# Attention followed by two MLPs: the first weight's conversion is spread differently, and one small addition changes engine

## The chip, the cores and the metric

The kernel runs on one core of a Trainium2 chip. The metric is the device time of one execution in microseconds (us). The kernel before took 933.87 us (median of three runs, 932.76 to 934.47). The profile shown here belongs to one execution that took 932.79 us.

The core has four compute engines with a queue of instructions each, and each works through its own queue in order: TensorE (PE; its weight loads are listed as PEld), VectorE (DVE), ScalarE (ACT) and GpSimd (POOL). SyncE (SP) only issues transfers (DMA). Instructions of different engines wait for one another by semaphores. SBUF is the on-chip memory, PSUM the memory that TensorE writes.

## The reference

Causal attention with a decaying bias for 4 batches of 8 heads (576 positions, 64 wide), and then two MLPs on the 2304 tokens:

```
sp = maximum(s, 0); cum = cumsum(sp)
scores = q @ k.T / 8 + minimum(-(cum_i - cum_j), 0), causal mask -1e9
a = exp(scores - max); a = a / (sum(a) + 1e-9); x = a @ v
h = x @ w1_in;  x = relu(h)**2 @ w1_out
h = x @ w2_in;  out = maximum(0.01*h, h) @ w2_out
```

x is 2304 by 512, the weights are 512 by 2048 and 2048 by 512. q, k, v, s and the result are float32; the weights arrive as float64 and are brought to float32 on the chip.

## The kernel before

**Attention in slots.** `attention` runs over 16 pairs of heads. Each pair has seven slots (`STEPS`): two for the first 256 query rows, two each for the third and the fourth 128, and one for the last 64 of both heads. `scores` (L469, L457) multiplies on TensorE into the PSUM tiles S and h; `maxima` (L488) masks and takes the row extreme on VectorE; `exponentials` (L512) runs on ScalarE and also gives the row sums; `flip` (L527) transposes on TensorE, and its results are copied out of PSUM as pT and pX by ScalarE (L550) or VectorE (L548); `values` (L569) multiplies with v; `gather` (L579) copies the result out as xo.

**The division.** `inverse` (L583) adds 1e-9 to the sums (L585), takes the reciprocal (L586), both on VectorE, and spreads it with a GpSimd copy into ex (L589). `spread` (L604) turns that on TensorE, and `scale` (L610, L614) multiplies xo on VectorE. The first five pairs do this in two portions (of 4 and 5 sums), the others in one (of 9). `store` (L755) writes xo to xscr.

**The first weight.** A float64 is read as two 32-bit words, a low and a high one, and a chunk of w1_in is a tile wst of 128 by 512 by 2 words. `load_w` has it fetched (L154), and three slots later works on it in three steps. ScalarE scales the high and the low word (L114, L115); VectorE masks and shifts (L117) and puts sign bits in (L120); GpSimd adds the low part (L122). Then ScalarE (from chunk 10 on VectorE, L171) makes the rounded copy (L169), and GpSimd the remainder (L172). There are 16 chunks, two tiles wst and two tiles wt, so that a chunk's transfer waits until the chunk two before it has left its tile. The slot in which chunk fc begins is the sum 11 + 5 fc // 2, and 4 more from chunk 8 on. The work of chunk 0 falls on slots 14 to 16, in pair 2 (slots 14 to 20).

**The first MLP's product beside attention.** From slot 35 (the start of pair 5) on, units of x @ w1_in (`up1`, L661) stand on TensorE's queue between the attention's matmuls, spread evenly over the slots.

**What sets the order.** TensorE's order in attention is fixed by `in_order`. On the other engines the order is made at the build from the program's order, priorities and an estimate of when each instruction can begin. It is then fixed: an instruction that waits holds all that stand behind it on its engine.

Of the kernel before, what the change touches and what calls it, by code (L numbers as in the profile page):

```python
# [12 lines left out]
AF = mybir.ActivationFunctionType  # L13
ALU = mybir.AluOpType
# [4 lines left out]
def f32(ap):  # L19
    return ap.bitcast(F32)  # L20
# [3 lines left out]
def attention_then_two_mlps(  # L24
# [24 lines left out]
    nc = tc.nc  # L49
# [11 lines left out]
    CV = 11  # L61
# [12 lines left out]
    AHEAD = 20  # L74
    PLAIN = 5
    ALONE = 5
    KINDS = (0, 2, 3, 4)
    STEPS = ((0, 0), (0, 1), (2, 0), (2, 1), (3, 0), (3, 1), (4, 0))

# [28 lines left out]

        return [bank("h") for _ in range(2)] if n < AHEAD and n % 2 else two_banks()

    def words(t, st, adder=nc.gpsimd):

        lw, hw = st[:, :, 0], st[:, :, 1]
        nc.scalar.activation(f32(t), f32(hw), AF.Copy, scale=2.0 ** -112)  # L114
        nc.scalar.activation(lw, lw, AF.Copy, scale=2.0 ** -29)  # L115
        yield
        nc.vector.tensor_scalar(t, t, 0x07FFFFFF, 3, ALU.bitwise_and, ALU.logical_shift_left)  # L117
        if adder is nc.vector:
            nc.vector.tensor_tensor(t, t, lw, ALU.add)  # L119
        nc.vector.scalar_tensor_tensor(t, hw, 0xC0000000, t, ALU.bitwise_and, ALU.bitwise_or)  # L120
        if adder is not nc.vector:
            adder.tensor_tensor(t, t, lw, ALU.add)  # L122
        yield
# [34 lines left out]
    def load_w(fc, pool, stage, lo_engine=nc.gpsimd):  # L158

        st = stage.words()  # L160
        read_w(st, w1_in, fc, False)
        for _ in range(3):
            yield
        dst = pool.tile([P, 2, DM], F32R, tag=f"w{fc}", name=f"w{fc}")
        win[fc] = dst
        t = stage.word()
        yield from words(t, st)
        if fc < 10:
            nc.scalar.activation(dst[:, 0], f32(t), AF.Copy)  # L169
        else:  # L170
            nc.vector.tensor_copy(dst[:, 0], f32(t))  # L171
        lo_engine.tensor_tensor(dst[:, 1], f32(t), f32(dst[:, 0]), ALU.subtract)  # L172
# [273 lines left out]
    def scores(x, kind):  # L446

        p = pairs[x]
        p.sc[kind] = score_banks(len(KINDS) * x + KINDS.index(kind))
        if kind == 4:  # L450
# [130 lines left out]
    def inverse(at, x, a, z):  # L581

        p = pairs[x]  # L583
        cols = p.sums[:, 2 * a:min(2 * z, 9)]
        nc.vector.tensor_scalar(cols, cols, 1.0e-9, None, ALU.add)  # L585
        nc.vector.reciprocal(cols, cols)  # L586
        w = 2 * (min(z, 4) - a)
        p.ex = at.tile([P, w, 64], F32, tag="ex", name="ex")
        nc.gpsimd.tensor_copy(p.ex, p.sums[:, 2 * a:2 * a + w].unsqueeze(2).to_broadcast([P, w, 64]))  # L589
# [81 lines left out]
    def attention(at, mg, mx):  # L671
# [5 lines left out]
        def at_slot(y, f, *args):  # L677
            later.setdefault(y, []).append((f, args))
# [52 lines left out]
        for j in range(B):  # L731
            for c in range(KC):
                job = up1_x(mx, j, c, XS)
# [24 lines left out]
        for fc in range(FC):  # L758
            job = load_w(fc, wpool, stage)
            for gap in range(6):  # L760
                at_slot(CV + 5 * fc // 2 + (4 if fc > 7 else 0) + gap, step, job)
        for ch in range(BEFORE):
            job = convert(*divmod(ch, FC), stage, nc.sync, 3)
            for gap in range(6):
# [3 lines left out]
        def values_at(x, region):  # L768

            return 10 if region or ALONE <= x < len(pairs) - 1 else 5 if x < ALONE else 6  # L770

# [38 lines left out]
        for y in range(end + 14):  # L810
            x, st = divmod(y, n)
# [8 lines left out]
            for early in (True, False):  # L820
# [7 lines left out]
                for z in (y - LAG, y - 1):  # L828
                    zx, zs = divmod(z, n)
                    kind, e = STEPS[zs]  # L830
                    if early != (kind == 0 and zx < ALONE):
                        continue
                    if 0 <= z < end and (e or kind == 4) and (z == y - 1) == (kind == 3 and zx >= ALONE):
                        flip(at, zx, kind, [live.pop(i) for i in range(z - e, z + 1)])
# [340 lines left out]
```

## Time and profile before

| | |
|---|---|
| median of three runs | 933.87 us |
| the profiled execution, and its span | 932.79 us, 931.0 us |
| TensorE busy | 898.3 us (96% of the span) |
| VectorE busy | 705.7 us (76%) |
| ScalarE busy | 577.7 us (62%) |
| GpSimd busy | 179.9 us (19%) |

The page's second part shows the span in 40 slices of 23 us. TensorE reads 5, 8, 7, 8 tenths in the first four and 9 (90% or more) in nearly all others:

```profile
PE   5878999999999999999999999999999999999997
DVE  5888776876774267589897997787488697886964
ACT  4788876878886444365565556686577754444442
POOL 4357763344330001001112101001110000000000
```

A line of the timeline gives the start and the duration in us, the engine, the line of the program, the instruction, what it writes and reads, and in brackets how long its engine had been idle before it and what ended that. Instructions of one engine overlap a little at their ends, so that durations of neighbours can't simply be added.

### The profile page before, as it was taken

To read this page: it belongs to the slowest core of one execution; us is meant where nothing else is said; L and a number is where in the kernel's file an instruction comes from. 1 tells how busy PE (TensorE), PEld (TensorE's weight loads), DVE (VectorE), ACT (ScalarE), POOL (GpSimd) and SP (SyncE) were. 2 spreads that over 40 slices of the span, in tenths; PEclk is the share of its full clock that TensorE was granted. 3 is DMA by queue.
4 is the path that set the end of the run, shared out by engine and by line. 5 is a ranking of instruction groups with operands and counts; after the bars stand their busy time and mean duration, and the time that the engine had idled before them with its cause. 6 is when DMAs were issued, how large, how long until landed. Compare 5 with 4: busy or idle time off the path is not lost.

```text
span 931.0 us, 16390 instructions
## 1 busy us (share of the span) xinstructions
PE 898.3 (96%) x5902; PEld 809.0 (87%) x5902; DVE 705.7 (76%) x1286; ACT 577.7 (62%) x1076; POOL 179.9 (19%) x290
## 2 busy tenths in 40 slices
PE   5878999999999999999999999999999999999997
PEld 3646777777777778999999999999999999999997
DVE  5888776876774267589897997787488697886964
ACT  4788876878886444365565556686577754444442
POOL 4357763344330001001112101001110000000000
PEclk9999999999999999999999999999999999999999
DMA  9776849778763377948649326668768575627303
GB/s 164 172 184 153 217 145 230 219 204 245 227 203 106 99 239 274 316 163 269 228 132 363 128 96 201 218 221 304 256 205 299 187 254 149 182 57 208 86 13 55
DMA packets 229569, 178.48 MB, mean 192 GB/s; under 512 B 139600, under 2 KB 206352, under 8 KB 229488
## 3 DMA queue, kind: packets, MB, share of 16 engines
q1 hardware_dynamic: 192568, 105.13, 41.7%
q10 hardware_dynamic: 27048, 38.16, 11.3%
q0 software_dynamic: 9872, 34.15, 10.5%
q8 instruction: 46, 0.75, 0.3%
q14 instruction: 35, 0.29, 0.1%
HBM read 111.25 MB, written 66.13 MB: 191 GB/s over the span
## 4 chain that ended last, share of the span: by engine, by line
PE 53%; issue 13%; DVE 6%; DMA 6%; POOL 1%; ACT 1%; POOLq 0%; ACTq 0%; DVEq 0%; SPq 0%
PE q L877 30%; PE h L661 16%; DVE op L984 3%; PE tr L569 2%; DMA gp<-gscr 2%; PE S L469 2%; PE tr L527 1%; PE S L457 1%; DMA gp<-qscr 1%; DMA wst<-in_moe_w_in_dram 1%; DMA qscr<-post 1%; DVE gp L978 1%; DMA wst<-in_moe_w_out_dram 1%; DVE wt L119 0%; POOL zscr L1046 0%
## 5 line engine op out<-in xcount | busy, mean ns | idle before, releaser
L877 PE MATMUL q<-op,w 128*128 128x384 f32 x3024 | 527.9, 335 | 4.0 <-DVE op L984 2.7
L877 PEld LDWEIGHTS q<-op,w 128*128 128x128 f32 x3024 | 523.7, 188 | 7.9 <-DVE op L984 5.0
L983 ACT ACTIVATE op<-gp 128x768 fp32r<-128x768 f32 x189 | 158.3, 846 | 152.3 <-PE q L877 128.4
L661 PE MATMUL h<-xs,w 128*128 128x512 f32 (+1 forms) x960 | 211.5, 374 | 1.2 <-ACT gs L640 0.8
L984 DVE TENSOR_TENSOR op<-gp,op 128x768 fp32r<-128x768 f32 x189 | 178.0, 953 | 40.6 <-ACT op L983 39.4
L661 PEld LDWEIGHTS h<-xs,w 128*128 128x128 f32 x960 | 163.6, 189 | 38.0 <-issue 6.0
L512 ACT ACTIVATE t<-t,m 128x256 f32<-128x256 f32 (+4 forms) x134 | 76.1, 569 | 44.1 <-DVE m L488 39.2
L488 DVE CUSTOM_DVE_ANT_0 t<-S,mask 128x128 f32<-128x128 f32 (+4 forms) x119 | 49.5, 460 | 43.3 <-PE S L469 28.2
L640 ACT ACTIVATE gs<-h 128x512 f32<-128x512 f32 (+1 forms) x80 | 43.8, 549 | 47.3 <-PE h L661 46.8
L185 POOL DMA_DIRECT2D wscr<-wt x48 | 26.6, 555 | 231.2 <-DVE wt L120 227.4
L950 DVE TENSOR_TENSOR post<-q,post 128x768 f32<-128x768 f32 (+1 forms) x55 | 51.6, 940 | 15.1 <-PE q L877 14.7
L469 PE MATMUL S<-Y 64*128 64x128 f32 (+3 forms) x324 | 42.9, 372 | 14.0 <-DVE Y L427 8.0
L930 ACT ACTIVATE post<-q 128x768 f32<-128x768 f32 (+1 forms) x56 | 43.8, 782 | 12.6 <-PE q L877 12.5
L114 ACT ACTIVATE wt<-wst 128x512 f32<-128x512 f32 x64 | 42.3, 661 | 12.2 <-DMA wst<-in_moe_w_in_dram 5.9
L569 PE MATMUL tr<-pT,v 128*64 128x320 f32 (+3 forms) x384 | 46.8, 387 | 2.5 <-ACT pT L550 2.0
L120 DVE SCALAR_TENSOR_TENSOR wt<-wst,wt 128x512 uint32<-128x512 uint32 x64 | 48.1, 753 | 0.9
L527 PEld LDWEIGHTS tr<-ident,t 64*128 64x128 f32 x720 | 28.6, 140 | 20.5 <-issue 11.3
L910 ACT ACTIVATE post<-post 128x768 f32<-128x768 f32 x36 | 30.4, 846 | 25.5 <-DVE post L950 25.4
L117 DVE TENSOR_SCALAR wt<-wt 128x512 uint32<-128x512 uint32 x64 | 31.7, 496 | 18.2 <-ACT wt L114 18.1
L569 PEld LDWEIGHTS tr<-pT,v 128*64 128x64 f32 x384 | 24.9, 137 | 23.1 <-issue 4.2
L115 ACT ACTIVATE wst<-wst 128x512 uint32<-128x512 uint32 x64 | 42.9, 670 | 2.7 <-DMA wst<-in_moe_w_out_dram 1.8
L198 DVE TENSOR_TENSOR w<-wq,w 128x512 fp32r<-128x512 f32 x49 | 33.3, 688 | 14.2 <-ACT w L197 13.9
(119 smaller groups left out, 943.7 us busy)
## 6 DMA issues: line engine op xcount, KB each, us to landing
gscr<-gs ACTq DMA_DIRECT2D x36, 512.0 KB
gp<-gscr SPq DMA_DIRECT2D x48, 384.0 KB
qscr<-post ACTq DMA_DIRECT2D x48, 384.0 KB
gp<-qscr SPq DMA_DIRECT2D x48, 384.0 KB
wscr<-wt POOLq DMA_DIRECT2D x48, 256.0 KB, 4.5
wst<-in_moe_w_in_dram SPq DMA_DIRECT2D x19, 512.0 KB
wst<-in_moe_w_out_dram SPq DMA_DIRECT2D x16, 512.0 KB
wst<-in_moe_w_out_dram POOLq DMA_DIRECT2D x16, 512.0 KB, 5.1
```

What stands on the lines that cost most here:

```text
L120: nc.vector.scalar_tensor_tensor(t, hw, 0xC0000000, t, ALU.bitwise_and, ALU.bitwise_or)
L469: nc.tensor.matmul(p.sc[kind][e][:, a:z], qs[hs, T * P:(T + 1) * P], ks[hs, :z - a], start=(n == 0 and y == 0), stop=(n == len(tiles) - 1 ...
L488: return nc.vector.tensor_tensor_reduce(t[:, a:z], sc, msk, -QK_SCALE, first, ALU.add, ALU.min, m).ins
L512: done = nc.scalar.activation(t[:, a:z], t[:, a:z], AF.Exp, bias=m[:, c:c + 1], scale=-1.0, accum_out=sums[:, s0:s0 + 1])
L569: p.anchor = nc.tensor.matmul(po[64 * e:64 * e + 64, a:n], p.vr[:, c, e], rhs[e], start=(y == 0), stop=(y == len(mm) - 1), skip_group_chec ...
L640: done = nc.scalar.activation(g, h[:, :w], AF.Relu)
L661: nc.tensor.matmul(h[:, :w], win[fc][:, a, c * P:(c + 1) * P], xs[j, c][:, z, :w], start=(c == 0 and y == 0), stop=(c == KC - 1 and y == 2))
L877: i = nc.tensor.matmul(*args, skip_group_check=True, **kw).ins
L930: done = nc.scalar.activation(t[:, xs], acc, AF.Copy)
L950: done = nc.vector.tensor_tensor(t[:, xs], acc, t[:, xs], ALU.add)
L983: a = nc.scalar.activation(t[:, 0], src, AF.Copy)
L984: c = nc.vector.tensor_tensor(t[:, 1], src, f32(t[:, 0]), ALU.subtract)
```

## The change

Three things change. First, the addition of 1e-9 in `inverse` goes from VectorE to ScalarE, for all pairs. Second, chunks 0 to 2 (`CALM`) have their high word scaled by GpSimd instead of ScalarE, and their rounded copy made by GpSimd (`lo_engine`) instead of ScalarE. Third, the slots: chunks 0, 1, 2 begin in slots 3, 7, 11 (before 11, 13, 16), chunk 3 in slot 17 (before 18), chunks 4 to 15 in 20, 22, 25, 28, 31, 33, 36, 39, 42, 44, 47, 50 (before 21, 23, 26, 28, 35, 37, 40, 42, 45, 47, 50, 52). What is computed stays.

```diff
+    CALM = 3
...
-    def words(t, st, adder=nc.gpsimd):
+    def words(t, st, adder=nc.gpsimd, calm=False):
...
-        nc.scalar.activation(f32(t), f32(hw), AF.Copy, scale=2.0 ** -112)
+        if calm:
+            nc.gpsimd.tensor_scalar(f32(t), f32(hw), 2.0 ** -112, None, ALU.mult)
+        else:
+            nc.scalar.activation(f32(t), f32(hw), AF.Copy, scale=2.0 ** -112)
         nc.scalar.activation(lw, lw, AF.Copy, scale=2.0 ** -29)
...
-        yield from words(t, st)
-        if fc < 10:
+        yield from words(t, st, nc.gpsimd, fc < CALM)
+        if fc < CALM:
+            lo_engine.tensor_copy(dst[:, 0], f32(t))
+        elif fc < 10:
             nc.scalar.activation(dst[:, 0], f32(t), AF.Copy)
...
-        nc.vector.tensor_scalar(cols, cols, 1.0e-9, None, ALU.add)
+        nc.scalar.activation(cols, cols, AF.Copy, bias=1.0e-9)
         nc.vector.reciprocal(cols, cols)
...
-                at_slot(CV + 5 * fc // 2 + (4 if fc > 7 else 0) + gap, step, job)
+                at_slot((4 * fc + 3 if fc < CALM else CV - 2 + 11 * fc // 4) + gap, step, job)
```

In the changed file the lines behind `words` have moved by 3 to 6: L116 is the GpSimd scaling, L119, L121, L124, L126 are the old L115, L117, L120, L122; L158 is the transfer (L154), L494 the maxima (L488), L591 the addition (L585), L592 the reciprocal (L586).

SP's queue, from the q and k of pairs 2 and 3 (kr, qr) on; v is a pair's values, ag its bias, wst a chunk of the weight. Before:

```order
L389 DMA qr<-in_q_dram 32x36x32 x4
L405 DMA v<-in_v_dram 128x4x64 x2
L407 DMA v<-in_v_dram 64x2x64
L405 DMA v<-in_v_dram 128x4x64 x2
L407 DMA v<-in_v_dram 64x2x64
L417 DMA ag_88<-aug 4x1152 x2
L154 DMA wst<-in_moe_w_in_dram 128x4x256 x2
```

and now:

```order
L395 DMA qr<-in_q_dram 32x36x32 x4
L411 DMA v<-in_v_dram 128x4x64 x2
L413 DMA v<-in_v_dram 64x2x64
L158 DMA wst<-in_moe_w_in_dram 128x4x256
L411 DMA v<-in_v_dram 128x4x64 x2
L413 DMA v<-in_v_dram 64x2x64
L158 DMA wst<-in_moe_w_in_dram 128x4x256
L423 DMA ag_88<-aug 4x1152 x2
```

The first chunk's transfer has moved up past one v and one ag, and stands right behind the first v.

VectorE's queue between the last maxima of pair 0 (h, 128x288) and the first of pair 1 (S, 128x128). Before:

```order
L488 ISA t,m<-h,mask_77,m 128x288
L488 ISA m 128x1
L585 TENSOR_SCALAR sums<-sums 128x5
L586 RECIPROCAL sums<-sums 128x5
L488 ISA t,m<-S,mask 128x128
```

and now:

```order
L494 ISA t,m<-h,mask_77,m 128x288
L494 ISA m 128x1
L592 RECIPROCAL sums<-sums 128x5
L121 TENSOR_SCALAR wt<-wt 128x512
L124 SCALAR_TENSOR_TENSOR wt<-wst,wt 128x512
L494 ISA t,m<-S,mask 128x128
```

The addition has gone, and the two instructions on chunk 0 stand ahead of the first maxima of pair 1. L121 waits for GpSimd's L116, and that for the chunk's transfer.

ScalarE's queue at the end of pair 2, from the exponentials of its fourth tile (Y) on. Before:

```order
L512 ACTIVATE Y,sums<-Y,m 128x512 x2
L114 ACTIVATE wt<-wst 128x512
L115 ACTIVATE wst<-wst 128x512
L579 ACTIVATE xo<-tr 128x256
L550 ACTIVATE pT_678<-tr 128x2x3x64 x2
L512 ACTIVATE t,sums<-t,m 128x576
```

and now:

```order
L518 ACTIVATE Y,sums<-Y,m 128x512
L118 ACTIVATE wt<-wst 128x512
L119 ACTIVATE wst<-wst 128x512
L518 ACTIVATE t,sums<-t,m 128x576
L585 ACTIVATE xo<-tr 128x256
L556 ACTIVATE pT_687<-tr 128x2x3x64
L591 ACTIVATE sums<-sums 128x5
L556 ACTIVATE pT_687<-tr 128x2x3x64
```

The last exponentials (128x576) now come before xo and pT; the addition stands behind xo and one copy of pT. The chunk scaled here was chunk 2 and is now chunk 3.

## Rows read from the trace of the kernel before

**Rows 1.** Stretches: busy us by engine, clock, DMA share, GB/s; when attention is full.
```profile
100.00:120.00 20.00, 20.00 (x168) 15.24 (x167) 15.09 (x40) 16.34 (x40) 13.47 (x16) 1.00 0.76 198
...
280.00:318.00 38.00, 38.00 (x295) 28.95 (x292) 15.14 (x51) 20.87 (x49) 2.79 (x4) 1.00 0.31 100
```

**Rows 2.** Timeline of VectorE: the first maxima of pairs 1 to 5.
```profile
22.63 0.29 DVE L488 CUSTOM_DVE_ANT_0 t<-S,mask 128x128 f32<-128x128 f32 x1 [2.95 <-PE S L469]
...
34.78 0.29 DVE L488 CUSTOM_DVE_ANT_0 t<-S,mask 128x128 f32<-128x128 f32 x1 [1.85 <-PE S L469]
...
49.43 0.25 DVE L488 CUSTOM_DVE_ANT_0 t<-S,mask 128x128 f32<-128x128 f32 x1
...
64.81 0.28 DVE L488 CUSTOM_DVE_ANT_0 t<-S,mask 128x128 f32<-128x128 f32 x1
...
78.48 0.28 DVE L488 CUSTOM_DVE_ANT_0 t<-S,mask 128x128 f32<-128x128 f32 x1
```

**Rows 3.** Timeline of SP's queue: some of the transfers that it issues.
```profile
20.50 0.64 SPq L407 DMA_DIRECT2D v<-in_v_dram  x1
...
24.32 0.85 SPq L417 DMA_DIRECT2D ag<-aug  x2
...
41.65 0.38 SPq L154 DMA_DIRECT2D wst<-in_moe_w_in_dram  x1
...
49.29 0.38 SPq L154 DMA_DIRECT2D wst<-in_moe_w_in_dram  x1
```

**Rows 4.** Timeline: the instructions that waited for three of these transfers.
```profile
26.52 0.55 POOL L442 CAST last<-ag 4x64 fp32r<-4x64 f32 x2 [10.10 <-DMA ag<-aug]
...
45.65 0.68 ACT L114 ACTIVATE wt<-wst 128x512 f32<-128x512 f32 x1 [1.51 <-DMA wst<-in_moe_w_in_dram]
...
54.03 0.69 ACT L114 ACTIVATE wt<-wst 128x512 f32<-128x512 f32 x1 [0.61 <-DMA wst<-in_moe_w_in_dram]
```

**Rows 5.** Timeline of GpSimd: instructions on 128 by 512.
```profile
40.32 1.30 POOL L122 TENSOR_TENSOR wt<-wt,wst 128x512 uint32<-128x512 uint32 x1 [1.75 <-ACT pT L550]
...
61.84 2.50 POOL L172 TENSOR_TENSOR w<-wt,w 128x512 fp32r<-128x512 f32 x2
...
98.81 0.61 POOL L589 COPY ex<-sums 128x512 f32<-128x512 f32 x1
```

**Rows 6.** Timeline of VectorE in pairs 1 and 2: chunk work, and a wait for TensorE.
```profile
30.39 0.46 DVE L488 CUSTOM_DVE_ANT_0 t<-h,mask 128x288 f32<-128x288 f32 x1 [0.44 <-PE h L457]
...
35.90 0.42 DVE L117 TENSOR_SCALAR wt<-wt 128x512 uint32<-128x512 uint32 x1
...
43.54 0.73 DVE L120 SCALAR_TENSOR_TENSOR wt<-wst,wt 128x512 uint32<-128x512 uint32 x1
```

**Rows 7.** Stretch with the lowered clock; columns as in rows 1.
```profile
20.00:24.00 4.00, 3.52 (x46) 2.89 (x45) 1.37 (x9) 1.74 (x7) 0.00 (x0) 0.78 0.85 176
```

**Rows 8.** Timeline of ScalarE: a small activation, the end of pair 2, pair 3's end.
```profile
4.15 0.20 ACT L695 ACTIVATE warm<-warm 128x1 f32<-128x1 f32 x1
...
46.80 0.36 ACT L579 ACTIVATE xo<-tr 128x256 f32<-128x256 f32 x1
...
47.80 0.77 ACT L512 ACTIVATE t<-t,m 128x576 f32<-128x576 f32 x1
...
61.77 0.63 ACT L617 ACTIVATE xs<-xh 128x512 fp32r<-128x512 f32 x1
```

**Rows 9.** Timeline of VectorE: the additions of 1e-9, and one subtraction.
```profile
48.70 0.59 DVE L585 TENSOR_SCALAR sums<-sums 128x5 f32<-128x5 f32 x1 [1.18 <-ACT t L512]
...
61.91 1.23 DVE L585 TENSOR_SCALAR sums<-sums 128x5 f32<-128x5 f32 x1 [1.71 <-ACT t L512]
...
63.28 1.60 DVE L618 TENSOR_TENSOR xs<-xh,xs 128x512 fp32r<-128x512 f32 x1
...
70.69 1.19 DVE L585 TENSOR_SCALAR sums<-sums 128x4 f32<-128x4 f32 x1
```

**Rows 10.** Timeline of TensorE in pair 5: its longest wait for VectorE.
```profile
83.71 2.16 PE L569 MATMUL tr<-pT,v 128*64 128x320 f32 x16 [0.41 <-DVE pT L548]
```

## The prediction

> **What bounds the kernel now.** I read the busy time by stretches first, then the timeline from the start, engine by engine. From 100 us to the end of attention TensorE is busy all the time: 20.00 of 20.00 us in the first stretch shown, 38.00 of 38.00 in the last [rows 1]. There VectorE, ScalarE and GpSimd have room, and what is taken off or put on them changes nothing as long as TensorE's queue stays fed. But the units of x @ w1_in that fill it begin only with pair 5, in a fixed order. So whatever moves the start of pair 5 moves all that follows by as much, and the question is what happens before 78.48 us.
>
> The first maxima of pairs 1 to 5 stand at 22.63, 34.78, 49.43, 64.81 and 78.48 us [rows 2]. The periods are 12.15 us for pair 1, which converts no chunk, and 14.65, 15.38 and 13.67 for pairs 2 to 4, which convert three, three and two. The reader is to see two things in them. In the middle of a pair VectorE works without a gap, so that a chunk's two instructions there push it. And between two pairs runs a chain through the last exponentials, the addition, the reciprocal and the next maxima, on which the additions sometimes take 1.19 and 1.23 us [rows 9] for four or five numbers.
>
> **Pair 0 to pair 1: chunk 0.** The change puts L121 and L124 of chunk 0 ahead of pair 1's first maxima. They wait for GpSimd's L116, and that for the transfer, which is issued behind the v that ends at 20.50 + 0.64 = 21.14 us [rows 3]. Nothing that stands before it on SP's queue has changed. Two chunk transfers with a wait behind them show how long landing takes: issued at 41.65, waited for until 45.65, 4.00 us; and 49.29 to 54.03, 4.74 us [rows 3, 4]. A transfer of some kilobytes took 24.32 to 26.52, 2.20 us, the lower bound. I take 4.00, the undisturbed one of the two: landed at 25.14. L116 is not in the trace: GpSimd's one-source copy of the same 128 by 512 took 0.61 us, its two-source addition 1.30 [rows 5]. It has one source, so 0.61: 25.75. L121 and L124 cost 0.42 and 0.73 [rows 6]: 26.90 instead of 22.63, or 4.3 us late. The bounds are 21.14 + 2.20 + 0.61 + 1.15 = 25.10 (2.5 late) and 21.14 + 4.74 + 1.30 + 1.15 = 28.33 (5.7 late). ScalarE stops in the same place (L119 waits for the transfer too, ahead of two copies of pT and of pair 1's exponentials), but then has only L119 (0.68 for its twin [rows 4]) and the copies (1.0 with xo in pair 2 [rows 8]) to do: 25.14 + 1.68 = 26.82, no later than VectorE. GpSimd's second L116 waits for chunk 1, and behind it stand chunk 0's addition and an ex that TensorE wants only in the second half of pair 1; that I cost at nothing.
>
> TensorE idles through this. In this place it already runs at less than its full 2.4 GHz: the granted clock is 0.78 in the stretch of 20 to 24 us, that is partly at 1.2 GHz, [rows 7], after a start in which TensorE was busy for 5 tenths only (the first slice of the page). More idle time may bring another such stretch. In these 4 us the lower clock cost 0.22 x 4.00 = 0.9 us of TensorE's time, twice that would be 1.8; but what follows the stall is bounded by VectorE, so I take 0.3, bounds 0 and 1.8.
>
> **Pair 1: chunk 1.** Its L121 and L124 come into the part where VectorE is full: 1.15 us. A wait of 0.44 for TensorE that stands behind them [rows 6] absorbs that much, 0.7 is left, and an overlap with GpSimd (below) may hold L121 for up to 1.30. I take 0.8, bounds 0.3 and 1.6.
>
> **Pair 2.** It loses chunk 1's two instructions from its full part, 1.15 us; chunk 2 takes chunk 0's place and chunk 3 that of chunk 2. Its last exponentials start at 47.80, behind xo and two copies that began at 46.80 [rows 8]; they now stand ahead of these, 1.0 us earlier. The addition took 0.59 instead of about 0.17, 0.4 us. Against that stands the addition on ScalarE, where the smallest activation shown takes 0.20 [rows 8], behind xo and a copy. 1.15 + 1.0 + 0.4 - 0.2 = 2.35; I take 2.4. More than 2.5 would bring the pair below pair 1's 12.15. The lower end is 1.2: chunk 3's transfer can be as late as chunk 2's was (1.51 us of waiting [rows 4]), and then ScalarE is held ahead of the last exponentials.
>
> **Pair 3.** The addition at 61.91 took 1.23 us and ended at 63.14, when the first of GpSimd's two L172 ended (61.84 and half of 2.50 [rows 5, 9]). VectorE waited for GpSimd to finish. Behind it stand the reciprocal and the subtraction xs (63.28, 1.60), which ended 0.47 after the second L172 (64.34), and then pair 4's maxima at 64.81. Without the addition the subtraction can be asked for when ScalarE's copy ends, 61.77 + 0.63 = 62.40 [rows 8]. If it then waits for the first L172 only, it runs from 63.1 to 63.8: 1.0 gained, which I take. Bounds: 0 (it still waits for both), and 1.7 (it runs at once).
>
> The Trainium skill, "SBUF — State Buffer", section "Who interferes with whom", says that VectorE and GpSimd share a pair of ports under an exclusive lock, and that the one that comes second blocks for the whole instruction. The trace agrees here: the 1.23 us ended with the L172. By that rule six more GpSimd instructions on chunks 0 to 2 are six more chances to be held, and taking away one VectorE instruction hands the wait to the next that needs the port; that is the second rival.
>
> **Pair 4 and pair 5.** In pair 4 the addition at 70.69 took 1.19 us within work without a gap [rows 9]; with the reciprocal in the place it has now, 1.1 is gained, bounds 0 and 1.2. In pair 5 TensorE already has the units. Its longest wait for VectorE there is 0.41 [rows 10], so the gain is at most about that: I take 0.3, bounds -0.6 (ScalarE, loaded there, gets the addition too) and 0.6. From pair 6 on I cost the additions and the moved chunks at nothing: TensorE's work covers them, and if that cover is gone in some pair, 0.2 us per pair appear, for eleven pairs 2.2.
>
> **The sum.** 4.3 + 0.3 + 0.8 - 2.4 - 1.0 - 1.1 - 0.3 = +0.6 us. On the profiled execution, 932.79 (its span of 931.0 and 1.79 around it), that is 933.4; the median of the runs shown lies 1.08 higher, so the median predicted is 933.87 + 0.6 = 934.5. I call less than 0.2% (1.87 us) no change, for that is about what a measurement of this kernel can tell: the forecast is no change that can be told.
>
> **The rivals.**
>
> First, faster: pairs 2 to 4 fall to pair 1's period. With a chunk gone from pair 2, the held additions gone, and the waits behind them with these, the three periods shrink by 2.5, 3.2 and 1.5, in sum 7.2, and the net is 4.3 + 0.3 + 0.8 - 7.2 - 0.3 = -2.1: 931.8. For it speaks that the waits sit at the pairs' ends and not in the work; against it, that pairs 3 and 4 keep three and two chunks. Chance 0.20. It decides from 5.4 + 1.87 = 7.3 us of gain in pairs 2 to 5 on.
>
> Second, slower: the hold moves and is not removed. In pair 3 the subtraction waits for both L172 whether the addition stands before it or not, and in pair 4 the next VectorE instruction that needs the port waits in the addition's place; pairs 3 and 4 then gain nothing, and the sum is 4.3 + 0.3 + 0.8 - 2.4 - 0.3 = +2.7: 936.6. For it speaks that the subtraction was held until the second L172 right behind the addition; against it, that the addition in pair 4 stands in a row of instructions of which others ran freely. It decides once 1.3 of the 2.1 us are not gained. Chance 0.30, with the few cases in which the stall alone, at 5.7, does as much.
>
> Third, the change doesn't do what it says, or rather does it better than the queue suggests: the first chunk is there in time and pair 1 starts at 22.63. Then the sum is 0.8 - 2.4 - 1.0 - 1.1 - 0.3 = -4.0, or 929.9. Against it stands the issue at 21.14, which the rows fix; even the shortest landing shown leaves 2.5 us. Chance 0.03.
>
> **How the numbers follow.** No change has 0.47, slower 0.30 and faster 0.23 (0.20 + 0.03). If all terms sat at their ends the sum would run from -3.2 (2.5 + 0 + 0.3 - 2.5 - 1.7 - 1.2 - 0.6) to 8.5 (5.7 + 1.8 + 1.6 - 1.2 + 0.6); they won't do so together, and the two large rivals give 931.8 and 936.6. Reaching beyond both by the half-width of the stall, about 1.6, gives 930.8 and 938.2, with about 1 in 10 left out on either side.
>
> **What would show it.** In the changed trace the first maxima of pair 1 (L494) should start near 26.9, with an idle VectorE before L121 that ended with GpSimd's L116, and GpSimd's and ScalarE's idle time there ended by the transfer of wst. The period of pair 1 should be near 13, of pair 2 near 12.3, of pair 3 near 14.4, of pair 4 near 12.6, and pair 5 should start about 0.9 us later than 78.48. Additions (L591) should take about 0.2 on ScalarE. From 100 us on TensorE should stay full and attention's end be shifted by about as much as pair 5. If pair 1 starts before 25 the main term is wrong; if pair 5 starts earlier than 76.5 or later than 81, the sum is; if its start is as forecast and the time is not, something behind attention moved, which I have taken as fixed.

## The result and the profile after

The changed kernel took 939.41 us (median; 937.84 to 940.35), the kernel before 933.27 us beside it: a ratio of 1.0068, 95% interval 1.0051 to 1.0085. It is 6.1 us slower. The forecast was 934.5 us, no change, with a range up to 938.2; the result lies outside. The profiled execution has a span of 937.3 us (before 931.0).

From the fifth slice on TensorE reads 9, as before; what is new lies in the first four, where its busy share is lower in two and higher in one, and its clock reads 8 in two. The second part of the page after:

```profile
PE   4698999999999999999999999999999999999997
DVE  5778765877784348489798998788488788786974
PEclk9898999999999999999999999999999999999999
```

The rows at the start of pair 1, from the timeline of the changed kernel (start, duration, engine, line, instruction, and in brackets the idle time ahead of it and what ended that). They answer to the issue of [rows 3] and the first maxima of [rows 2]:

```profile
21.21 1.46 SPq L158 DMA_DIRECT2D wst<-in_moe_w_in_dram  x1
26.28 0.65 ACT L119 ACTIVATE wst<-wst 128x512 uint32<-128x512 uint32 x1 [6.66 <-DMA wst<-in_moe_w_in_dram]
26.43 1.51 POOL L116 TENSOR_SCALAR wt<-wst 128x512 f32<-128x512 f32 x1 [10.00 <-DMA wst<-in_moe_w_in_dram]
27.98 0.43 DVE L121 TENSOR_SCALAR wt<-wt 128x512 uint32<-128x512 uint32 x1 [8.13 <-POOL wt L116]
28.44 0.69 DVE L124 SCALAR_TENSOR_TENSOR wt<-wst,wt 128x512 uint32<-128x512 uint32 x1
29.05 0.28 DVE L494 CUSTOM_DVE_ANT_0 t<-S,mask 128x128 f32<-128x128 f32 x1
```

The reader follows one chain down: the transfer is issued at 21.21 and waited for until 26.28, GpSimd scales for 1.51 us, VectorE works on chunk 0, and only then come pair 1's maxima, 6.42 us later than the 22.63 of before. VectorE had been idle for 8.13 us. The first maxima of pairs 2 to 5 after, in the same view:

```profile
41.16 0.29 DVE L494 CUSTOM_DVE_ANT_0 t<-S,mask 128x128 f32<-128x128 f32 x1 [0.18 <-PE S L475]
56.31 0.25 DVE L494 CUSTOM_DVE_ANT_0 t<-S,mask 128x128 f32<-128x128 f32 x1
70.32 0.28 DVE L494 CUSTOM_DVE_ANT_0 t<-S,mask 128x128 f32<-128x128 f32 x1
83.36 0.29 DVE L494 CUSTOM_DVE_ANT_0 t<-S,mask 128x128 f32<-128x128 f32 x1
```

The periods are 12.11, 15.15, 14.01 and 13.04 us (before 12.15, 14.65, 15.38, 13.67), so pairs 1 to 4 give back only 1.5 of the 6.4 us. Pair 5 starts 4.88 us late and the span is 6.3 longer; 1.4 more is lost behind pair 5's start. TensorE's clock in stretches after the stall and in pair 4 (stretch; TensorE busy; granted clock; DMA share; GB/s):

```profile
28.00:32.00 4.00, 2.24 (x15) 0.50 0.08 25
32.00:36.00 4.00, 4.00 (x36) 0.80 0.42 130
48.00:52.00 4.00, 4.00 (x24) 0.67 0.88 186
72.00:76.00 4.00, 4.00 (x22) 0.50 0.92 188
```

At 0.50 it is at 1.2 GHz for the whole stretch. In pair 2 this and the next transfer eat the gain (changed kernel, timeline; first the issues on SP's queue):

```profile
40.65 3.40 SPq L395 DMA_DIRECT2D kr<-in_k_dram  x4
44.10 4.45 SPq L395 DMA_DIRECT2D qr<-in_q_dram  x4
48.65 1.21 SPq L158 DMA_DIRECT2D wst<-in_moe_w_in_dram  x2
51.60 0.46 DVE L494 CUSTOM_DVE_ANT_0 t<-h,mask 128x288 f32<-128x288 f32 x1 [1.60 <-PE h L463]
53.43 0.67 ACT L118 ACTIVATE wt<-wst 128x512 f32<-128x512 f32 x1 [1.50 <-DMA wst<-in_moe_w_in_dram]
54.57 0.77 ACT L518 ACTIVATE t<-t,m 128x576 f32<-128x576 f32 x1
```

VectorE waits 1.60 us for TensorE, in the stretch with a clock of 0.67, and ScalarE 1.50 us for chunk 3's transfer, whose scaling stands ahead of the pair's last exponentials. That transfer is issued only at 48.65, behind the eight loads of k and q.

### The profile page after: what moved, and what is told of

It reads as the page before. It is cut to its first block, busy times and chain, and to the rows that moved or that the text cites. A ratio compares the mean times of both kernels' runs of the same rounds, so it can differ in the third digit from the quotient of the medians.

```text
span 937.3 us, 16356 instructions
## 1 busy us (share of the span) xinstructions
PE 902.4 (96%) x5902; PEld 810.3 (86%) x5902; DVE 701.5 (75%) x1265; ACT 577.2 (62%) x1091; POOL 185.5 (20%) x296
## 4 chain that ended last, share of the span: by engine, by line
PE 65%; issue 10%; DVE 10%; DMA 8%; ACT 3%; POOL 2%; SPq 1%; POOLq 0%; DVEq 0%; ACTq 0%
PE q L883 33%; PE h L667 20%; PE tr L575 4%; PE S L475 3%; DVE op L990 3%; PE tr L533 3%; DMA wst<-in_moe_w_in_dram 2%; PE S L463 1%; DMA gp<-gscr 1%; DMA gp<-zscr 1%; DVE gp L984 1%; DMA zscr<-post 1%; DVE t L494 1%; PE tr L610 1%; DVE wt L124 1%
## 5 line engine op out<-in xcount | busy, mean ns | idle before, releaser
L494 DVE CUSTOM_DVE_ANT_0 t<-S,mask 128x128 f32<-128x128 f32 (+4 forms) x119 | 49.4, 459 | 38.9 <-PE S L475 25.6
L575 PE MATMUL tr<-pT,v 128*64 128x320 f32 (+3 forms) x384 | 49.0, 401 | 3.1 <-ACT pT L556 2.0
L936 ACT ACTIVATE post<-q 128x768 f32<-128x768 f32 (+1 forms) x56 | 43.7, 781 | 12.8 <-PE q L883 12.6
L124 DVE SCALAR_TENSOR_TENSOR wt<-wst,wt 128x512 uint32<-128x512 uint32 x64 | 50.9, 795 | 0.9
L121 DVE TENSOR_SCALAR wt<-wt 128x512 uint32<-128x512 uint32 x64 | 30.7, 480 | 27.6 <-ACT wt L118 19.4
L119 ACT ACTIVATE wst<-wst 128x512 uint32<-128x512 uint32 x64 | 42.9, 671 | 9.4 <-DMA wst<-in_moe_w_in_dram 7.5
L118 ACT ACTIVATE wt<-wst 128x512 f32<-128x512 f32 x61 | 40.3, 660 | 11.7 <-DMA wst<-in_moe_w_in_dram 7.0
L533 PE MATMUL tr<-ident,t 64*128 64x64 f32 x720 | 37.6, 234 | 7.8 <-ACT pT L556 5.8
```

The costliest lines, as they stand in the source:

```text
L494: return nc.vector.tensor_tensor_reduce(t[:, a:z], sc, msk, -QK_SCALE, first, ALU.add, ALU.min, m).ins
L533: nc.tensor.transpose(banks[r][:, 64 * n:64 * n + 64], t[hs, a:a + P], ident[hs, hs])
L575: p.anchor = nc.tensor.matmul(po[64 * e:64 * e + 64, a:n], p.vr[:, c, e], rhs[e], start=(y == 0), stop=(y == len(mm) - 1), skip_group_chec ...
```

## The experiments

Each time is a median, each ratio against runs of the kernel before on the same chip. The last three columns are the first maxima of pairs 1, 5 and 7 in the profiled execution, read as in [rows 2].

| run | edit | us | ratio (95%) | pair 1 | pair 5 | pair 7 |
|---|---|---|---|---|---|---|
| before | | 932 to 933 | 1 | 22.63 | 78.48 | 119.81 |
| after | the change | 939.41 | 1.0068 (1.0051-1.0085) | 29.05 | 83.36 | 126.72 |
| e1 | after, early chunks worked on later | 938.98 | 1.0073 (1.0048-1.0098) | 21.25 | 78.91 | 124.14 |
| e2 | after, chunks 0-2 in old slots | 942.57 | 1.0116 (1.0098-1.0134) | 22.12 | 80.46 | 131.01 |
| e3 | after, no GpSimd scaling and copy | 937.50 | 1.0069 (1.0044-1.0093) | 27.45 | 82.59 | 125.72 |
| e4 | before, addition on ScalarE | 931.09 | 0.9997 (0.9982-1.0012) | 20.71 | 75.12 | 117.43 |
| e5 | before, later spacing alone | 937.09 | 1.0056 (1.0039-1.0072) | 22.70 | 78.09 | 124.90 |
| e6 | before, GpSimd alone | 940.17 | 1.0084 (1.0066-1.0102) | 22.70 | 77.78 | 125.47 |
| e7 | before, early slots alone | 938.06 | 1.0070 (1.0053-1.0087) | 28.20 | 83.42 | 124.23 |
| e8 | after, old later spacing | 939.70 | 1.0083 (1.0064-1.0101) | 29.57 | 83.66 | 125.34 |
| e9 | e4, chunk 9 one slot later | 930.33 | 0.9991 (0.9973-1.0009) | 20.90 | 76.11 | 117.52 |
| e10 | e4, chunk 9 two slots later | 932.86 | 1.0011 (0.9995-1.0027) | 21.11 | 75.48 | 119.16 |
| e11 | e1, chunk 7 one slot later | 938.46 | 1.0067 (1.0045-1.0089) | 22.36 | 82.05 | 125.90 |
| e12 | after, chunk 0 by ScalarE's queue | 937.87 | 1.0065 (1.0043-1.0086) | 21.72 | 82.32 | 125.30 |
| e13 | before, 2 transfers instead of 16 | 929.49 | 0.9968 (0.9953-0.9983) | 22.24 | 74.23 | 115.42 |
| e14 | after, 2 transfers instead of 16 | 936.47 | 1.0049 (1.0030-1.0068) | 28.16 | 81.00 | 121.67 |
| e15 | after, chunks 0-2 by ScalarE's queue | 938.01 | 1.0060 (1.0041-1.0080) | 25.32 | 80.47 | 123.92 |
| e16 | after, all by ScalarE's queue | 934.62 | 1.0030 (1.0015-1.0044) | 24.94 | 79.66 | 121.33 |
| e17 | after, no transfer | 931.59 | 0.9989 (0.9974-1.0004) | 23.70 | 76.73 | 117.51 |
| e18 | e4, all by ScalarE's queue | 930.97 | 0.9986 (0.9967-1.0006) | 20.80 | 76.18 | 117.96 |

The last column sorts the times into groups: kernels whose pair 7 starts before 120 us take 929 to 933 us, those after 123.9 us 937 to 943 us, and e14 and e16 lie between. Nearly all is decided before pair 7; pair 1's column alone does not decide it.

**e1, the stall taken away by working later on the chunks.**

```diff
-                at_slot((4 * fc + 3 if fc < CALM else CV - 2 + 11 * fc // 4) + gap, step, job)
+                at_slot((4 * fc + 3 + 4 * (gap > 2) if fc < CALM else CV - 2 + 11 * fc // 4) + gap, step, job)
```

> The changed kernel, with one difference: the six steps that convert each of the first three chunks run four slots later, while the chunk's transfer stays where the change put it. So GpSimd still scales and copies, the addition is still on ScalarE, and the transfer is still issued at about 21 us; but no step of chunk 0 stands ahead of pair 1's first maxima. T1 (the whole loss is the stall between pair 0 and pair 1: the transfer's landing and the 1.51 us scaling in front of those maxima): the first maxima of pair 1 come back from 29.05 to between 22.6 and 23.5 us, so 6 us are given back there, and the time is 939.4 - 6.0 = 933.4 us, at most 1 us either way for what chunks 0 to 2 now do inside pairs 1 to 3. R1 (the loss is GpSimd's two new operations of 1.51 and 0.61 us, which hold VectorE's L121 and L124 in every one of the pairs): those operations are all still there, so pair 1 starts early but the periods of pairs 1 to 3 grow by about as much, and the time stays at 937 us or above. R2 (the lowered TensorE clock of 28 to 36 and 44 to 52 us): if the clock falls without the stall too, 2 to 3 us of the 6 remain, and the time is 935.5 to 936.5 us.

Pair 1 starts at 21.25, as T1 wanted, and the time stays. The timeline of e1 in pair 1:

```profile
28.86 1.55 POOL L116 TENSOR_SCALAR wt<-wst 128x512 f32<-128x512 f32 x1 [1.59 <-DMA wst<-in_moe_w_in_dram]
31.40 0.44 PE L610 MATMUL tr<-ident,ex 128*128 128x128 f32 x2 [1.81 <-POOL ex L595]
36.75 0.29 DVE L494 CUSTOM_DVE_ANT_0 t<-S,mask 128x128 f32<-128x128 f32 x1 [3.26 <-PE S L475]
```

GpSimd now waits for chunk 1's transfer with ex behind it, and TensorE waits for ex: pair 1 takes 15.50 us instead of 12.11. The wait has moved. Pair 5 takes 25.83 us (before 21.15).

**e2 and e3: old slots; ScalarE instead of GpSimd.** In e2 the first expression of the slot line is `CV + 5 * fc // 2`; e3 has

```diff
-        yield from words(t, st, nc.gpsimd, fc < CALM)
-        if fc < CALM:
-            lo_engine.tensor_copy(dst[:, 0], f32(t))
-        elif fc < 10:
+        yield from words(t, st)
+        if fc < 10:
             nc.scalar.activation(dst[:, 0], f32(t), AF.Copy)
...
```

> The changed kernel, with the first three chunks begun in the slots that they had before (11, 13 and 16) instead of 3, 7 and 11; GpSimd's scaling and copy, the addition on ScalarE and the later chunks' spacing are kept. T1 (stall between pair 0 and pair 1): no chunk work stands there, the first maxima of pair 1 come at 22.6 us, and the time is that of before or a little less: 931 to 933.5 us, the little from the addition on ScalarE, whose 0.59 and 1.23 us on VectorE go. R1 (GpSimd's operations cost the time wherever they stand): three scalings of 1.51 us and three copies of 0.61 us now stand in pairs 2 and 3 together with the halves' subtractions, VectorE is held there, and the time is 936 us or more.

> The changed kernel with the scaling and the copy of the first three chunks back on ScalarE; the early slots, the addition on ScalarE and the later spacing are kept. T1 (stall: waiting for the landing 5.07 us after the issue, then the scaling): the landing stays, ScalarE's scaling takes 0.6 to 0.7 us where GpSimd's took 1.51, so the first maxima of pair 1 come about 0.85 us earlier, at 28.2 us, and the time is 938.6 us; the stall itself stays at about 5.5 us. R1 (GpSimd's operations are the loss): with all of them gone the time comes back to 934 us or below.

e2 has no stall at pair 1 and is the slowest of all: T1, that the stall is the whole, falls as it stood. e3 starts pair 1 1.6 us earlier, and its ratio is that of the changed kernel: GpSimd's operations are not the main part there. Why e2 is slower still was not isolated; its pairs 5 and 6 take 25.43 and 25.12 us.

**e4 to e8: one part at a time.**

```diff
-        nc.vector.tensor_scalar(cols, cols, 1.0e-9, None, ALU.add)
+        nc.scalar.activation(cols, cols, AF.Copy, bias=1.0e-9)
```

> The kernel before with one part of the change: the addition to the sums goes from VectorE to ScalarE; the chunks stay in their slots and on their engines. T1: the addition has no part in the loss; on VectorE it stood in the end of pairs 2, 3 and 4 with 0.59 to 1.23 us behind a held subtraction, on ScalarE it takes 0.2 us, so the time is 0 to 2 us below before: 931.3 to 933.3 us. R3 (the addition on ScalarE queues behind the last exponentials and the reciprocal then waits for another engine, 0.9 us in pair 2 of the changed kernel, in each of the 9 pairs or so): 2 us or more above before, 935 us and more.

For e5 to e8 the slot expression is, in turn:

```diff
+ (CV + 5 * fc // 2 if fc < 3 else CV - 2 + 11 * fc // 4)
+ CV + 5 * fc // 2 + (4 if fc > 7 else 0)
+ (4 * fc + 3 if fc < 3 else CV + 5 * fc // 2 + (4 if fc > 7 else 0))
+ (4 * fc + 3 if fc < CALM else CV + 5 * fc // 2 + (4 if fc > 7 else 0))
```

> The kernel before with one part of the change: chunks 3 to 15 begin every 2.75 slots (17, 20, 22, 25, 28, 31, 33, ...) as in the changed kernel; chunks 0 to 2 stay in slots 11, 13 and 16 and on ScalarE, the addition stays on VectorE. The last three runs with the 2.75 spacing are 0.7 to 1.2% slow whether the stall between pairs 0 and 1 is there or not, and the addition alone gave 0.9997, so the stall cannot be the whole. T2 (the later chunks' new spacing is the loss: their steps then stand between the last subtraction of one pair and the first maxima of the next): pair 1 starts as before, and the time is 6 to 10 us over before, 938 to 942 us. R1 (GpSimd's scaling and copies are the loss): no such operation is here, so the time is that of before within 1.5 us.

> The kernel before with one part of the change: GpSimd scales (1.51 us) and copies (0.61 us) chunks 0 to 2, in their old slots 11, 13 and 16; all other chunks in their old slots, the addition on VectorE. R1 (GpSimd's operations hold VectorE and are the loss): 6 to 10 us over before. T2 (the spacing of the later chunks is the loss): within 2 us of before, since three times 1.51 + 0.61 - 0.66 - 0.66 us of one chain that is read only by the later filling cost little.

> The kernel before with one part of the change: chunks 0 to 2 begin in slots 3, 7 and 11; ScalarE scales and copies them, the other chunks keep their slots, the addition stays on VectorE. The stall at the start of pair 1 is here as in the changed kernel, without GpSimd's scaling: first maxima at 26.5 to 28.2 us. T1 (that stall goes to the end): about +4 us, 936 us. T2 (the loss is the later spacing; pairs 2 and 3 without chunks 0 to 2 give back what the stall takes): within 2 us of before.

> The changed kernel with one part undone: chunks 3 to 15 go back to their old slots (18, 21, 23, 26, 28, then 35, 37, 40, ...); chunks 0 to 2 still come at 3, 7 and 11 with GpSimd's scaling and copies, the addition is on ScalarE. T2 (the spacing is the loss): the stall of 6 us at pair 1's start is here and yet the time falls by 5 to 9 us from the changed kernel, to 930 to 934 us, since the pairs from 2 on are freer. T1 with R1 (stall and GpSimd): it stays at 937 to 940 us.

The addition alone does nothing that can be told. Each other part alone costs 5 to 8 us, about as much as all together: the parts don't add up. e6 and e8 come out where R1 had them, but e5 and e7 lose 5 to 6 us without any GpSimd scaling, and e8 keeps the loss without the later spacing, so neither R1 nor T2 is the whole. e7 and e8 have the stall. e5 and e6 start pair 5 as early as before and lose their time in it (25.59 and 26.35 us instead of 21.15). In e6 the build has put two chunks' instructions between pair 5's last maxima and pair 6's first (timeline of e6; one L124 and others between are left out):

```profile
98.57 0.57 DVE L121 TENSOR_SCALAR wt<-wt 128x512 uint32<-128x512 uint32 x1 [2.98 <-ACT wt L118]
100.47 1.46 DVE L121 TENSOR_SCALAR wt<-wt 128x512 uint32<-128x512 uint32 x1 [0.23 <-ACT wt L118]
103.05 1.16 DVE L124 SCALAR_TENSOR_TENSOR wt<-wst,wt 128x512 uint32<-128x512 uint32 x1
104.13 0.28 DVE L494 CUSTOM_DVE_ANT_0 t<-S,mask 128x128 f32<-128x128 f32 x1
```

**e9 to e11: is that place the cost?** In e9 and e10 `(1 if fc == 9 and gap > 2 else 0)`, and 2 for e10, is added to the slot in e4; in e11 `(1 if fc == 7 else 0)` to the later chunks' slot in e1.

> The kernel before with the addition on ScalarE (0.9997 of before when run alone), and one step more: the conversion of chunk 9 begins one slot later. On VectorE this moves only two instructions of that chunk (mask and sign, 0.43 and 0.69 us) from ahead of the last two maxima of pair 5 to behind them, so ahead of the first maxima of pair 6. T3 (the build's order puts a chunk's two instructions between the last maxima of one pair and the first of the next, TensorE has nothing to do there, and that is lost time): the 3.3 us from pair 5's last maxima to pair 6's first become 5 to 7 us, and the time rises by 2 to 4 us, to 933 to 935 us. Rival R4 (TensorE's queue is full from pair 5 on, so what VectorE does there is covered): 931 us, no change.

> As the run before it, but the conversion of chunk 9 begins two slots later, which puts its instructions into the middle of pair 6, behind the first maxima. T3: the 3.3 us between pair 5 and pair 6 stay, and the time is that of the kernel with the addition alone, 931 us within 1 us. R5 (any shift of one chunk disturbs the order as much): 2 to 4 us slower, as the run before it.

> The changed kernel with the first three chunks' conversion four slots later (no stall ahead of pair 1; that alone gave 938.98 us, 1.0073), and chunk 7 one slot later. The second edit clears the stretch between pair 5 and pair 6 of the two conversion instructions that the build had put there, where that run spent 6.46 us instead of 3.19. T1 with T3 (the stall and the conversions between pairs are the loss; both are gone here): pair 1 starts at 21 to 22.7 us, the stretch takes about 3.3 us, and the time is 932 to 935 us. R5 (chunks 0 to 2 inside pairs 1 to 3 and GpSimd's operations are the loss): it stays at 938 to 939 us.

e9 (timeline; the lines between are left out):

```profile
92.47 0.43 DVE L117 TENSOR_SCALAR wt<-wt 128x512 uint32<-128x512 uint32 x1 [1.03 <-ACT wt L114]
92.93 1.68 DVE L120 SCALAR_TENSOR_TENSOR wt<-wst,wt 128x512 uint32<-128x512 uint32 x1
97.37 0.28 DVE L488 CUSTOM_DVE_ANT_0 t<-S,mask 128x128 f32<-128x128 f32 x1
```

One chunk's instructions stand between the pairs, the stretch is 6.46 us instead of 3.31 in e4, and the time is unchanged: for one chunk R4 holds and T3 falls. In e10 the time does not change either. e11 clears the place (the stretch is 4.83 us there) and gains nothing; its pair 2 takes 16.43 us, with VectorE waiting 4.18 us for chunk 3.

**e12: the first transfer from another queue.**

```diff
-        read_w(st, w1_in, fc, False)
+        read_w(st, w1_in, fc, False, nc.scalar if fc == 0 else nc.sync)
```

> The changed kernel with one difference: the transfer of chunk 0 is issued on ScalarE's queue, amid the exponentials of pair 0 (about 15 us), and not on SyncE's at 21.21 us behind the loads of q, k and v. L121 and L124 of chunk 0 still stand ahead of pair 1's first maxima. T1 (the wait for the landing is the stall): landed at 20 to 21 us, VectorE waits no more, pair 1 starts at 23.5 to 24.5 us instead of 29.05, and the time is 4 to 5 us less than the changed kernel's, 934 to 935.5 us. Rival R6 (the stall is hidden behind something that is late anyway, and the loss is the spacing and GpSimd): 938 to 940 us. A part of the gain can go where the transfer, five microseconds earlier, takes the place of q and k of the next pairs.

Pair 1 starts at 21.72, 7.3 us earlier than in the changed kernel, and takes 20.15 us (timeline of e12):

```profile
26.33 0.60 SPq L158 DMA_DIRECT2D wst<-in_moe_w_in_dram  x1
30.63 0.67 ACT L119 ACTIVATE wst<-wst 128x512 uint32<-128x512 uint32 x1 [6.15 <-DMA wst<-in_moe_w_in_dram]
32.24 0.43 DVE L121 TENSOR_SCALAR wt<-wt 128x512 uint32<-128x512 uint32 x1 [4.93 <-POOL wt L116]
35.20 0.69 PE L610 MATMUL tr<-ident,ex 128*128 128x128 f32 x2 [5.18 <-POOL ex L595]
```

The same chain as at pair 1's start, one chunk on. The time gained at one place is spent at the next.

**e13, e14 and e17: the transfers taken away.** Two tiles serve all 16 chunks; in e17 they are filled on the chip instead of loaded.

```diff
-        st = stage.words()
-        read_w(st, w1_in, fc, False)
+        st = kept[fc % 2]
...
```

> The kernel before without the chunks' transfers: two tiles of the first weight are loaded once at the start of attention, and all 16 chunks are converted from these two, so that 14 transfers of 0.5 MB, and all waiting for them, are left out (the first MLP then works on other weights; every other operation stays). T7 (the late transfers hold ScalarE and VectorE): the kernel before lost 3.2 us of ScalarE to them, of which part shows: 928 to 931 us. It is the base for the next run.

> The changed kernel without the chunks' transfers, as in the run before it. T7 (what all slower kernels share is that chunks are worked on before their transfer has landed, and the engines behind stand still; where in the pairs that falls is secondary): the time falls by 8 to 11 us to that of the run before it, within 2 us, or below it. R1 with R5 (GpSimd's longer operations, or the order at large): those are all still here, so the distance between the two stays at 5 to 8 us.

> The changed kernel without any transfer of the first weight's chunks: two tiles are filled on the chip early in pair 0 (two GpSimd fills and two copies of two columns), and all 16 chunks are converted from these; every conversion step is still there, in the changed slots and on the changed engines. T8 (in the first pairs the transfers come out of DMA engines that are busy for 0.9 of the time, so that a chunk converted that early is waited for, or something else is, and that alone is the loss): pair 1 starts at 21 to 23.5 us, and the time is that of the kernel before without its transfers, 929.5 us, within 2 us. R1 with R5 (GpSimd's operations and the order have a share): 932 to 936 us.

In e14 the first load was still issued late, and the chain is that of the changed kernel (timeline of e14):

```profile
20.95 1.88 SPq L159 DMA_DIRECT2D wst<-in_moe_w_in_dram  x2
25.54 1.51 POOL L117 TENSOR_SCALAR wt<-wst 128x512 f32<-128x512 f32 x1 [9.47 <-DMA wst<-in_moe_w_in_dram]
27.08 0.43 DVE L122 TENSOR_SCALAR wt<-wt 128x512 uint32<-128x512 uint32 x1 [7.59 <-POOL wt L117]
28.16 0.28 DVE L494 CUSTOM_DVE_ANT_0 t<-S,mask 128x128 f32<-128x128 f32 x1
```

e14 lies 7.0 us above e13: 5.9 of them stand at the start of pair 1 (28.16 against 22.24) and are still there at pair 7 (6.25). T7 expected the two to meet; they did not, because one wait was left. e17 takes that one away (timeline of e17):

```profile
18.83 0.42 DVE L122 TENSOR_SCALAR wt<-wt 128x512 uint32<-128x512 uint32 x1
19.29 0.69 DVE L125 SCALAR_TENSOR_TENSOR wt<-wst,wt 128x512 uint32<-128x512 uint32 x1
23.70 0.29 DVE L498 CUSTOM_DVE_ANT_0 t<-S,mask 128x128 f32<-128x128 f32 x1 [2.23 <-PE S L479]
```

VectorE's two instructions stand in the same place, run without a wait, and VectorE then waits 2.23 us for TensorE as it did before. The time is 931.59, 4.9 us below e14 (their intervals, 0.9974 to 1.0004 and 1.0030 to 1.0068, don't meet) and 2.1 above e13. Of the 2.1, 1.37 us is the later start of pair 0 (11.67 against 10.30), where VectorE's first scaling took 1.98 us beside GpSimd's fills (0.45 in e14). So with the slots, engines and order of the change kept, 0.7 us remain. Against the forecasts, 931.59 lies 0.1 above T8's bound and 0.4 below that of R1 with R5; less the share of this run's own fills it is T8's, and R1 and R5 have no share that can be told.

**e15, e16 and e18: other queues for more transfers.** The queue is `nc.scalar` for chunks 0 to 2 in e15, for all in e16 and e18.

> The changed kernel with the transfers of chunks 0 to 2 issued from ScalarE's queue and not from SyncE's, where loads of q, k and v for later pairs stand ahead of them. With chunk 0 alone moved, pair 1 began at 21.72 us, but then chunk 1 (issued by SyncE at 26.33, landed at 30.6) held pair 1 for 20.15 us. T7: with chunks 0 to 2 in time, pair 1 starts at 21 to 23, its period is 12 to 13.5 us, and the time is 2 to 6 us below the changed kernel's, 933.5 to 937 us (chunks 3 to 15 still come late). R6 (SyncE's queue is not what makes them late, the landing is): the waits stay, 937 to 940 us.

> The changed kernel with all 16 chunks' transfers issued from ScalarE's queue. T7 with SyncE's queue as the cause of the lateness: a further 1 to 3 us below the run before it, 931 to 935 us. R6 (the landing itself is slow, or ScalarE's queue issues them no earlier): as the run before it or slower, since each issue now takes 0.4 to 0.6 us of ScalarE's time.

> The kernel before with the addition on ScalarE and with all 16 transfers of the first weight issued from ScalarE's queue. Without its transfers the kernel before came to 929.5 us, so no way of issuing them should go below that by more than the noise. T8: 929.5 to 932 us, a little below before if chunk 2's transfer (1.5 us of waiting in pair 2) comes earlier, no gain if an issue of 0.4 us on ScalarE stands ahead of exponentials. R6: slower than before by 1 to 3 us, since ScalarE now spends 16 times 0.4 us on issuing.

Timeline of e16 around the start of pair 1:

```profile
13.00 4.50 SPq L395 DMA_DIRECT2D kr<-in_k_dram  x4
13.48 0.40 ACTq L158 DMA_DIRECT2D wst<-in_moe_w_in_dram  x1
20.72 1.27 SPq L411 DMA_DIRECT2D v<-in_v_dram  x2
24.33 0.38 ACT L585 ACTIVATE xo<-tr 128x256 f32<-128x256 f32 x1 [4.52 <-DMA v<-in_v_dram]
24.94 0.25 DVE L494 CUSTOM_DVE_ANT_0 t<-S,mask 128x128 f32<-128x128 f32 x1
```

Chunk 0 is on time, but the four loads of k beside it take 4.50 us to issue (2.56 in the kernel before), v is issued 1.65 us later than before (20.72 against 19.07), and now v is what ScalarE waits for. In the kernel before the DMA share of that stretch was already full (length, busy time of PE, PEld, DVE, ACT and POOL, the clock, the DMA share, GB/s; below it the issues of k and v from the timeline of before):

```profile
10.00:20.00 10.00, 7.50 (x56) 4.82 (x57) 6.31 (x26) 6.80 (x22) 2.98 (x13) 0.92 1.02 186
13.21 2.56 SPq L389 DMA_DIRECT2D kr<-in_k_dram  x4
19.07 1.39 SPq L405 DMA_DIRECT2D v<-in_v_dram  x2
```

So at pair 1's start the wait became smaller and changed its place, but did not go (24.94, against 29.05 in the changed kernel and 22.63 before): 512 kB more in a stretch whose share is 1.02 come out of something else there. The Trainium skill, "DMA: Bandwidth & Descriptors", section "Issuing engines are not separate DMA queues", says that transfers of all issuing engines run on the same 16 DMA engines and interleave, and that another issuer saves only the time of issuing; the 4.50 us for k agree with that.

With all transfers from ScalarE's queue the changed kernel takes 934.62 us, a ratio of 1.0030 against 1.0068: about half of the loss is back, and the time is in T7's range. In pair 2 the queue matters (timeline of e16, the issue and the scaling of chunk 3):

```profile
40.10 0.38 ACTq L158 DMA_DIRECT2D wst<-in_moe_w_in_dram  x1
46.70 0.68 ACT L118 ACTIVATE wt<-wst 128x512 f32<-128x512 f32 x1
```

Chunk 3 is issued 8.55 us earlier than in the changed kernel (pair 2 begins 3.45 earlier), nothing waits for it, and pair 2 takes 12.65 us instead of 15.15. In e15 SyncE still issues chunk 3 behind k and q, at 45.67; ScalarE waits 3.34 us for it, pair 2 takes 15.28, and the time of 938.01 is in R6's range and not in T7's. Against e15, e16 is 0.8 us ahead at pair 5 and 2.6 at pair 7. On the kernel before the same step (e18) changes nothing that can be told, and leaving out 14 of the 16 transfers (e13) gives 0.3%: the transfers cost less there. No version is faster than the kernel before by more than the measurement tells, except e13, which leaves most transfers out.

## Why the prediction was wrong

**What bounds.** Right: what is lost before pair 7 goes to the end nearly one to one (e14 against e13: 5.9 at pair 1, 7.0 in the time). The bound the prediction did not weigh is the DMA engines' share of the first pairs and, in pair 2, the place of chunk 3's transfer on SyncE's queue. It placed chunk 0's transfer by that queue and took its landing from a transfer in pair 2.

**Pair 0 to pair 1 (+4.3 forecast, +6.42 measured).** The mechanism and the order were right, as was the issue (21.14 forecast, 21.21). Two sizes were off: landing took 5.07 us, not 4.00, and L116 took 1.51, not 0.61. That is 1.14 later with the issue, 0.15 before GpSimd starts, and 0.90 for L116, less 0.04 behind it: 2.15, the whole difference between 26.90 and 29.05. L116 even lies above its upper bound of 1.30. The value was drawn from a copy of adjacent words, while L116 reads every second word; but the addition behind the bound reads every second word of one source too, so what makes L116 dearer than that stays open.

**Pair 1 (+0.8; measured -0.04)** and the clock (+0.3; not visible in that pair though the clock was 0.50): too pessimistic by 1.1.

**Pair 2 (-2.4; measured +0.50).** This is the step that failed most, with 2.9 us. Its lower end, -1.2, named the danger (chunk 3's transfer late, ahead of the last exponentials), and 1.50 us of that came; 1.60 us of waiting for TensorE came beside it, in a stretch with a clock of 0.67. Without transfers the pair takes 12.62 us with three chunks in it (e13) and 12.64 with two (e17), and 12.74 in e14, which has the stall; the granted clock is 1.00 from 44 to 52 us in e13, e14 and e17. So what the pair took over 12.6 us came with the transfers, before and after the change, and of the 2.4 us forecast (less chunk work, exponentials earlier, the addition gone) nothing shows between e13 and e17.

**Pairs 3 and 4 (-1.0 and -1.1; measured -1.37 and -0.63).** The sum, -2.0, is right; that it is right is in part luck. In pair 3 the subtraction ended at 70.39, soon after the first of GpSimd's two remainders (68.57 and half of 2.96) and not after the second, as forecast. In pair 4 L121 and L124 took 1.34 and 1.48 us (0.42 and 0.66 at 64.35 and 63.77 in pair 3); before, it was the addition with 1.19 and an L117 with 1.69. So two instructions took long there as before, which is what the second rival described, but it did not decide. The prediction counted three chunks in pair 3; the trace of before has VectorE work on two there (L117 at 54.98 and 55.92, the next at 67.67), and so has that of after. The addition alone (e4) shortens pair 3 by 1.56 us and changes the time by a ratio of 0.9997 (0.9982 to 1.0012), so it is not shown that the gain in these pairs reaches the time.

**From pair 5 on (-0.3; measured +1.4).** The cover of TensorE was not whole behind the late start: pair 5 takes 23.51 us (before 21.15), and 20.82 and 20.91 where the transfers are left out (e14, e17). The prediction's falsifier, a pair 5 later than 81 us, was met at 83.36.

Together: 2.1 + 2.9 - 1.1 + 0.1 + 1.7 = 5.7, the way from the forecast +0.6 to +6.3 in the span. The lower end of the range has a slip: 931.8 less 1.6 is 930.2, not 930.8; nothing hangs on it here.

**What was costed at nothing.** GpSimd's second L116 with ex behind it cost nothing in the changed kernel, but 1.81 us in e1 and 5.18 us in e12, as soon as the first stall was gone.

**What stays open.** That the early transfer's wait is most of the loss of the changed kernel is shown by e14 and e17: 4.9 of the 7.0 us between e14 and e13 go with it. Why the old slots (e2), the later spacing alone (e5) and GpSimd alone (e6) lose their time in pair 5 was not isolated. In e5 ScalarE waits 3.28 us for a chunk's transfer there; in e6 VectorE waits 1.93 and 2.98 us for scalings, the first of which stood behind a wait of ScalarE for GpSimd. None of the three was run without transfers; e9 shows that one chunk's instructions between the pairs are not enough.

## What to carry to other kernels

A step that is moved earlier takes its transfer with it: read the DMA share of the stretch where the transfer will go, and what stands ahead of it on the queue that issues it. Here moving the first one or three transfers to another queue gave nothing back, moving all sixteen about half. When removing a wait does not bring its time back, look for the next in-order instruction that waits for the same supply, and test by taking the supply's wait away with every instruction kept (e17), not by moving instructions one at a time. A cost for an operation is drawn from rows with the same operation and the same access to memory.

## What was not expected of the hardware

- GpSimd's scaling of 128x512 with every second word read took 1.51 to 1.55 us, against 0.61 for its copy of 128x512 adjacent words and 1.30 for its two-source addition, which reads every second word of one source [rows 5]; ScalarE does the same scaling in 0.66 on average.
- Issuing the same four loads of k took 2.56 us on SyncE's queue in the kernel before and 4.50 us with one 512 kB transfer issued beside them from ScalarE's queue (e16; 4.56 in e15, 5.33 in e12).
- After the stall the granted clock was 0.50 for a whole stretch of 4 us, and later 0.50 in a stretch in which TensorE was busy for 4.00 of 4.00 us.
